# Half rounds on TensorE: the values of one group between the second and third score chunk of the next

## The chip, the cores and the metric

The kernel runs on one core of a Trainium2 chip. Its engines are TensorE (PE: matmuls into PSUM, with weight loads, PEld, beside them), VectorE (DVE), ScalarE (ACT), GpSimd (POOL) and SyncE (SP), which issues nearly all loads here. The metric is the device time of one execution in microseconds. The kernel before took 665.82 us, the median of 3 runs (665.6 to 666.0). The profiled execution took 665.59 us; its span, from the first to the last instruction, was 664.4 us.

## The reference

Two attention blocks, A and B, of the same shape, each decode one token against a cache; their outputs stand side by side in one row of 1024.

```python
B, Sq, D = 1, 1, 512
H, Sk, Dh = 32, 8192, 128
q = (x @ wq).reshape(B, Sq, H, Dh).transpose(0, 2, 1, 3)
scores = einsum("bhqd,bhkd->bhqk", q, k_cache) * (Dh ** -0.5)
p = softmax(scores)
o = einsum("bhqk,bhkd->bhqd", p, v_cache)
out = o.transpose(0, 2, 1, 3).reshape(B, Sq, H * Dh) @ wo      # for A and for B
```

All arrays are bf16. The caches are 4 x 64 MB, the weights 4 x 4 MB, and each byte of them is used once.

## The kernel before, in words

The 64 heads (32 of A, then 32 of B) are worked off in 16 groups of four heads (NM = 16). For a group, the keys of four heads fill one half of `kn` (8 MB: 32 partitions per head, 256 key rows per partition, in four chunks of 64), and the values fill `vn` (8 MB). `kn` has two halves that alternate from group to group, `vn` has one.

**Scores.** Keys lie with the key rows on partitions, so the score is not a matmul over the head's dimension. DVE multiplies a chunk of keys by the broadcast query in place (L421, four per group, count `s_mul`). PE then adds up the products by identity matmuls into one PSUM bank per chunk: 16 matmuls of 512 columns, L253 and L256, which leave 8 partial sums per key. DVE reduces those to scores (L426, count `s_sr`), takes the maximum (L437, L445: `gm`), and ACT computes the exponentials into `pt` and their sums into `rsum` (L378 to L383, count `s_p`).

**Values.** PE sums `rsum` over partitions (L295), waits for the values (`s_v`), multiplies `pt` with them in 64 matmuls (L304, `acc`), and counts `s_pv`. ACT copies `acc` to SBUF (L376), PE selects the four heads' parts (L310, `tps`, count `s_turn`), and DVE scales them into `oD` (L442). The program calls group n's score chunks and the values of the group behind, n-1, one round.

**The order on PE.** PE runs a loop of 17 rounds. Round n does the four chunks of group n, each as soon as its multiply is done, and then the values of group n-1. In round 16 there are no chunks; their place takes the projection of the first 48 heads by `wo` (L263 to L292), and then come the values of group 15. After the loop the last heads of B are projected, four matmuls per head (L229, `yrow`), as their pieces of `wo` arrive.

**The order on DVE.** Per group: four multiplies, four reduces, maximum, reciprocal (needs the values' L295 of group n-1), the scaling into `oD` (needs `s_turn` of group n-1), `gm`. After the last group it spreads the outputs for the projection (L457) and copies what PE returns.

**The order of loads on SP** is one queue: keys n+1 wait for the first multiply of group n (`s_mul`), values n wait for the end of the values n-1 (`s_pv`), in turn:

```python
for n in range(2, NM - 1):
    load_k(n + 1, (s_mul, NCH * n + 1))
    load_v(n, (s_pv, n + 1))
load_wo(0, 0, H, s_woA, (s_mul, NCH * (NM - 1) + 1))
load_wo(1, *WOB[0], s_wo[0])
```

Then come the values of group 15, as 6 MB (`s_v`) and 2 MB (`s_v1`), after `s_pv` of group 14, and the rest of B's `wo` in pieces of 1 MB down to 128 KB.

Of the kernel before, what the change touches and what calls it, by code (L numbers as in the profile page):

```python
# [6 lines left out]
ALU = mybir.AluOpType  # L7
# [7 lines left out]
def bass_concat_heads__mha_block_cached__gqa_block_cached__decode_kernel(  # L15
# [31 lines left out]
    NM = NA * QA  # L47
# [4 lines left out]
    NCH = T // CT  # L52
# [15 lines left out]
    with ExitStack() as st:  # L68
# [5 lines left out]
        def flat(ap):  # L74
            return ap.rearrange("p t d -> p (t d)")
# [134 lines left out]
        def got_wo(e, g):  # L210
            e.wait_ge(s_wo[g], 16)


        e = nc.tensor
        rq = e.alloc_register("pe_rq")
        n1, k1, rv, ko = [e.alloc_register("pe_" + x) for x in ("n1", "k1", "rv", "ko")]
        nc.br("pe_first", engines=[nc.tensor.engine])
        with nc.body("pe_main", valid_engines=[nc.tensor.engine]):
            tp = Count(t_pe)

            def relayout(psv, z, n):
                return e.matmul(psv[:, 0:n], zb[:, z, :], jsel[n][:], start=True, stop=True)

            def rows(g):
                h0, n = WOB[g]
                for j in range(h0, h0 + n):
                    for i in range(NQ):
                        m = QR - QR * (i % 2) + i % 2
                        r = e.matmul(yrow[i * QR:i * QR + m, 0:P], oz[:, j - HT, QR - m:QR],  # L229
                                     wo_sb[:, H + j, i * P:(i + 1) * P], start=False,  # L230
                                     stop=(j == H - 1), skip_group_check=True)
                return r

            e.reg_mov(n1, 1)
            e.reg_mov(k1, 1)
            e.reg_mov(ko, 0)
            e.wait_ge(s_qc, 2 * NA * QA + QC)

            def chunk(off):
                v = e.snap(ko, min_val=0, max_val=2 * T * Dh - CT * Dh)  # L240
                return flat(kn[:])[:, bass.ds(v + off, CT * Dh)].rearrange(
                    "p (t d) -> p t d", d=Dh)[:, :, 0:DW]

            with e.Fori(0, NM + 1) as n:
                nr = e.alloc_register("pe_nr")
                e.reg_sub(nr, n1, 1)
                with e.If_lt(nr, NM):
                    with e.Fori(0, NCH) as c:
                        e.wait_ge(s_mul, k1)
                        e.wait_ge(s_sr, k1)  # L250
                        e.reg_add(k1, k1, 1)
                        o = big[:, bass.ds(c, 1), :].rearrange("p o (t d) -> p (o t) d", d=DW)
                        e.matmul(o, ident[:], chunk(0), start=True, stop=False, skip_group_check=True)  # L253
                        with e.Fori(0, RL):
                            for u in range(RU):
                                i = e.matmul(o, ident[:], chunk((1 + u) * DW), start=False,  # L256
                                             stop=(u == RU - 1), skip_group_check=True)
                            i.then_inc(s_red, 1)
                            e.reg_add(ko, ko, RU * DW)
                        e.reg_add(ko, ko, CT * Dh - RU * RL * DW)  # L260
                    e.reg_alu(ko, ko, 2 * T * Dh - 1, op=ALU.bitwise_and)
                with e.Else():
                    e.wait_ge(t_dve, 1)  # L263
                    tp.of(relayout(zps, 0, 32))
                    e.wait_ge(t_dve, 2)
                    tp.of(relayout(z2, 1, 16))
                    jo = e.alloc_register("pe_jo")
                    e.reg_mov(jo, 0)
                    for a, c in ((0, s_woA), (1, s_wo[0])):
                        y = big[0:1, a, :]  # L270
                        e.wait_ge(t_dve, 3 + a)
                        e.wait_ge(c, 16)
                        e.matmul(y, zero[:], wo_sb[:, 0, :], start=True, stop=False,
                                 skip_group_check=True)
                        with e.Fori(0, 8 - 4 * a):
                            h = e.snap(jo, min_val=0, max_val=H + HT - 4)
                            for u in range(4):
                                i = e.matmul(y, o2[:, bass.ds(h + u, 1)], wo_sb[:, h + u, :], start=False,  # L278
                                             stop=False, skip_group_check=True)
                            i.then_inc(s_y, 1)  # L280
                            e.reg_add(jo, jo, 4)
                    e.wait_ge(t_act, 2)
                    for i in range(NQ):
                        m = QR - 1 if i % 2 else 0
                        r = e.matmul(yrow[i * QR:(i + 1) * QR, 0:P], hot[:, m:m + QR],
                                     part[:, i * P:(i + 1) * P], start=True, stop=False,
                                     skip_group_check=True)
                    e.wait_ge(t_dve, 5)
                    tp.of(relayout(zps, 0, 8))
                    e.wait_ge(t_dve, 6)  # L290
                    tp.of(relayout(z2, 1, 4))
                    e.wait_ge(t_dve, 8)  # L292
                with e.If_ne(nr, 0):
                    e.wait_ge(s_p, n1)
                    e.matmul(misc[:, 0:G], ones_f[:], rsum[:], start=True, stop=True).then_inc(s_sum, 1)  # L295
                    e.reg_alu(rv, nr, 4, op=ALU.logical_shift_left)
                    e.wait_ge(s_v, rv)
                    for j in range(T // NT):
                        if j * NT == VCUT:
                            with e.If_eq(nr, NM):  # L300
                                e.wait_ge(s_v1, 16)
                        q = QB * (j % NP)
                        ts = slice(j * NT, (j + 1) * NT)
                        i = e.matmul(acc[q:q + NT * G, :], pt[:, ts, :].rearrange("p t g -> p (t g)"),  # L304
                                     vn[:, ts, :].rearrange("p t d -> p (t d)"), start=(j < NP),
                                     stop=(j >= T // NT - NP), skip_group_check=True)
                    i.then_inc(s_pv, 1)
                    e.wait_ge(s_acc, n1)
                    for t in range(NT):
                        i = e.matmul(tps[:, 0:G], acc_sb[:, t * Dh:(t + 1) * Dh],  # L310
                                     tsel[:, t * G:(t + 1) * G], start=(t == 0), stop=(t == NT - 1))
                    i.then_inc(s_turn, 1)
                e.reg_add(n1, n1, 1)
            got_wo(e, 1)
            rows(1)
            got_wo(e, 2)
            rows(2)
            e.wait_ge(t_dve, 9)
            for g in range(3, len(WOB)):
                got_wo(e, g)  # L320
                i = rows(g)
            tp.of(i)
            nc.br("pe_end", engines=[nc.tensor.engine])
# [32 lines left out]
        e = nc.scalar  # L356
        rq, n1 = [e.alloc_register("act_" + x) for x in ("rq", "n1")]
# [38 lines left out]
        e = nc.vector  # L396
        n1, k5, rk, kt, ks = [e.alloc_register("dve_" + x) for x in ("n1", "k5", "rk", "kt", "ks")]
# [16 lines left out]
        with e.Fori(0, NM):  # L414
            e.wait_ge(s_k, rk)
            kv = e.snap(kt, min_val=0, max_val=T)  # L416
            n = e.snap(n1, min_val=1, max_val=NM) - 1
# [100 lines left out]
```

## Time and profile before

| | before |
|---|---|
| median of 3 runs | 665.82 us (665.6 to 666.0) |
| profiled execution | 665.59 us, span 664.4 us |
| PE matmul, DVE, ACT busy | 60%, 51%, 12% of the span |
| DMA queue q1 | 285.22 MB, 99.4% of 16 engines' span |
| mean granted PE clock | 0.805 |
| chain of waits | DMA 82%, DVE 12%, issue 3%, PE 2% |

In the views of the profile a row of the timeline has the start and the length in us, the engine, the line, the operation, output and input; in brackets stands the idle time before and what ended it. A row of a stretch has start and end, its length, the busy time of PE, PEld, DVE, ACT and POOL with the count of instructions, the mean granted clock of PE (1.00 is full), the share of the 16 DMA engines, and GB/s. DMA shares over short stretches are uneven, since one packet is up to 64 KB. A row of DMA issues gives the size of one and the median time from issue to landing. The chain of waits gives start, length and what was waited for.

### The profile page before, as it was taken

How to read it: one execution, taken by the hardware profiler on the slowest of the kernel's cores; microseconds unless marked ns; L12 is line 12 of the kernel's file. 1: busy time of each engine (PE TensorE's matmuls, PEld its weight loads, DVE VectorE, ACT ScalarE, POOL GpSimd, SP SyncE). 2: the span in 40 equal slices, each digit the busy share in tenths (PEclk: the TensorE clock that was granted, in tenths of full speed). 3: DMA queues.
4: the chain of work that ended last, by engine and by line, in shares of the span. 5: the costliest groups of instructions: out<-in, count | busy, mean ns of one | idle time of the engine just before them, and what ended most of it. 6: DMA issues, size and time to landing. Idle time of an engine off the chain costs nothing.

```text
span 664.4 us, 8052 instructions
## 1 busy us (share of the span) xinstructions
PE 396.2 (60%) x2406; PEld 164.9 (25%) x2406; DVE 335.9 (51%) x213; ACT 80.9 (12%) x182; POOL 2.4 (0%) x13
## 2 busy tenths in 40 slices
PE   0739576739194673919467391946739194673986
PEld 0213232313032231303223130322313032231332
DVE  1047939356280935628093662809266380926600
ACT  1320211100202010020201002020100202010030
POOL 1000000000000000000000000000000000000000
PEclk9968796959688695958869595886959598695997
DMA  9999999999999999999999999999999999999998
GB/s 378 444 442 442 422 399 442 442 442 442 442 430 414 418 442 442 442 442 442 422 399 442 442 442 442 442 434 406 422 442 442 442 442 442 422 399 442 440 424 335
DMA packets 6207, 285.24 MB, mean 429 GB/s; under 512 B 699, under 2 KB 1214, under 8 KB 1342
## 3 DMA queue, kind: packets, MB, share of 16 engines
q1 hardware_dynamic: 6200, 285.22, 99.4%
q8 instruction: 1, 0.02, 0.0%
q10 hardware_dynamic: 6, 0.00, 0.0%
HBM read 285.21 MB, written 0.00 MB: 429 GB/s over the span
## 4 chain that ended last, share of the span: by engine, by line
DMA 82%; DVE 12%; issue 3%; PE 2%; SPq 1%; DVEq 0%
DMA kn<-in_B_k_cache_dram 41%; DMA kn<-in_A_k_cache_dram 37%; DVE kn L421 11%; DMA kn<-in_B_wo_dram 4%; PE big L256 1%; SPq L173 1%; PE acc L304 1%; DVE s_sb L426 0%; DVEq L416 0%; DVEq L421 0%; PE big L253 0%; PE misc L295 0%; DVE out_q L481 0%; PE yrow L229 0%; DVEq L429 0%
## 5 line engine op out<-in xcount | busy, mean ns | idle before, releaser
L421 DVE TENSOR_TENSOR kn<-kn,qbc x64 | 278.9, 4421 | 158.5 <-DMA kn<-in_A_k_cache_dram 86.6
L256 PE MATMUL big<-kn,ident 128*128 x960 | 267.9, 421 | 0.0
L253 PE MATMUL big<-kn,ident 128*128 x64 | 27.5, 429 | 223.7 <-DVE kn L421 209.8
L256 PEld LDWEIGHTS big<-kn,ident 128*128 128x128 bf16 x960 | 101.1, 105 | 152.9 <-issue 104.4
L426 DVE TENSOR_REDUCE s_sb<-big 128x64 f32<-128x512 f32 x64 | 41.2, 686 | 64.0 <-PE big L256 64.0
L376 ACT COPY acc_sb<-acc 128x512 f32<-128x512 f32 x16 | 9.4, 585 | 476.8 <-PE acc L304 476.7
L253 PEld LDWEIGHTS big<-kn,ident 128*128 128x128 bf16 x64 | 6.3, 98 | 239.4 <-issue 237.4
L304 PE MATMUL acc<-vn,pt 128*16 128x512 bf16 x1024 | 60.6, 391 | 2.9 <-DMA vn<-in_B_v_cache_dram 2.9
L382 ACT ACTIVATE pt<-s_sb,negb 32x256 bf16<-32x256 f32 x64 | 54.8, 856 | 1.3
L442 DVE TENSOR_TENSOR oD<-tps,rinv 128x4 f32 x16 | 2.6, 163 | 75.7 <-PE tps L310 75.5
L304 PEld LDWEIGHTS acc<-vn,pt 128*16 128x16 bf16 x1024 | 24.5, 91 | 31.3 <-issue 3.5
L310 PE MATMUL tps<-tsel,acc_sb 128*128 128x4 f32 x128 | 16.9, 255 | 11.0 <-ACT acc_sb L376 10.3
L346 PE MATMUL big<-vn,acc_sb 128*128 x64 | 16.7, 407 | 6.6 <-ACT qbc L371 3.6
L310 PEld LDWEIGHTS tps<-tsel,acc_sb 128*128 128x128 f32 x128 | 15.5, 191 | 19.1 <-ACT acc_sb L376 17.9
L382 ACT ACTIVATION_READ_ACCUMULATOR pt<-s_sb,negb 32x1 f32 x64 | 15.9, 248 | 0.0
L278 PE MATMUL big<-kn,o 128*1 x48 | 12.0, 377 | 0.0
L371 ACT CAST qbc<-big 32x512 f32 x16 | 9.2, 576 | 14.7 <-PE big L346 14.5
L346 PEld LDWEIGHTS big<-vn,acc_sb 128*128 x64 | 6.5, 102 | 16.5 <-issue 11.8
L295 PE MATMUL misc<-rsum,ones_f 128*128 128x4 f32 x32 | 6.0, 259 | 6.7 <-issue 6.1
L378 ACT ACTIVATE negb<-gm 128x1 f32<-128x1 f32 x16 | 3.2, 203 | 53.2 <-DVE gm L445 53.2
L332 PE MATMUL misc<-ones_bf,kn 1*128 1x128 bf16 x4 | 0.6, 302 | 13.2 <-DMA kn<-in_B_x_dram 13.2
L295 PEld LDWEIGHTS misc<-rsum,ones_f 128*128 128x128 f32 x32 | 4.8, 188 | 13.4 <-issue 13.4
(46 smaller groups left out, 36.0 us busy)
## 6 DMA issues: line engine op xcount, KB each, us to landing
vn<-in_B_v_cache_dram SPq DMA_DIRECT2D x1, 6144.0 KB, 20.6
vn<-in_A_wq_dram SPq DMA_DIRECT2D x1, 4096.0 KB, 12.4
vn<-in_B_wq_dram SPq DMA_DIRECT2D x1, 4096.0 KB, 21.4
kn<-in_A_wo_dram SPq DMA_DIRECT2D x1, 4096.0 KB, 24.3
kn<-in_B_wo_dram SPq DMA_DIRECT2D x1, 2048.0 KB, 28.9
vn<-in_B_v_cache_dram SPq DMA_DIRECT2D x1, 2048.0 KB, 25.2
kn<-in_B_wo_dram SPq DMA_DIRECT2D x1, 1024.0 KB, 27.2
kn<-in_B_wo_dram SPq DMA_DIRECT2D x1, 512.0 KB, 28.0
```

The costliest lines, as they stand in the source:

```text
L253: e.matmul(o, ident[:], chunk(0), start=True, stop=False, skip_group_check=True)
L256: i = e.matmul(o, ident[:], chunk((1 + u) * DW), start=False, stop=(u == RU - 1), skip_group_check=True)
L278: i = e.matmul(y, o2[:, bass.ds(h + u, 1)], wo_sb[:, h + u, :], start=False, stop=False, skip_group_check=True)
L295: e.matmul(misc[:, 0:G], ones_f[:], rsum[:], start=True, stop=True).then_inc(s_sum, 1)
L304: i = e.matmul(acc[q:q + NT * G, :], pt[:, ts, :].rearrange("p t g -> p (t g)"), vn[:, ts, :].rearrange("p t d -> p (t d)"), start=(j < NP ...
L310: i = e.matmul(tps[:, 0:G], acc_sb[:, t * Dh:(t + 1) * Dh], tsel[:, t * G:(t + 1) * G], start=(t == 0), stop=(t == NT - 1))
L346: i = e.matmul(big[:].rearrange("p (u v) (i d) -> p u v i d", v=2, d=Dh)[:, bass.ds(u, 1), v].rearrange("p o i d -> p (o i) d"), xb[:, a, ...
L371: e.copy(qbc[q, bass.ds(j * 4, 4), :].rearrange("p i d -> p (i d)"), big[q, hh, :]).then_inc(s_qc, 2)
L376: e.copy(acc_sb[:], acc).then_inc(s_acc, 1)
L382: i = e.activation(pt[q, :, h], s_sb[q, :], AF.Exp, bias=negb[q, :], scale=scale, accum_out=rsum[q, h:h + 1])
L421: e.tensor_tensor(k, k, qbc[:, bass.ds(n, 1), :].broadcast_to([P, CT, Dh]), ALU.mult).then_inc(s_mul, 1)
L426: e.tensor_reduce(s_sb[:, c * CT:(c + 1) * CT], big[:, c, :].rearrange("p (t d) -> p t d", d=DW), AX.X, ALU.add).then_inc(s_sr, 1)
```

## The change

PE's loop has 33 half rounds instead of 17 rounds. A half round does two score chunks. After every second half round but the first two, that is behind chunks 0 and 1 of group n, the values of group n-1 follow, and then chunks 2 and 3 of group n. The last half round holds the projection and the values of group 15, as the last round did. The counters that told the round (`nr`, `n1`) are now registers that are counted up: `cb` the bank, `rv` the count for the values, `odd` whether values follow. What is computed, the buffers and the other engines' programs stay as they were.

```diff
-            e.reg_mov(n1, 1)
+            e.reg_mov(n1, 2)
             e.reg_mov(k1, 1)
+            e.reg_mov(rv, 16)
             e.reg_mov(ko, 0)
+            e.reg_mov(cb, 0)
+            e.reg_mov(odd, 2)
...
-            with e.Fori(0, NM + 1) as n:
-                nr = e.alloc_register("pe_nr")
-                e.reg_sub(nr, n1, 1)
-                with e.If_lt(nr, NM):
-                    with e.Fori(0, NCH) as c:
+            with e.Fori(0, 2 * NM + 1):
+                with e.If_lt(k1, NCH * NM):
+                    with e.Fori(0, NCH // 2):
                         e.wait_ge(s_mul, k1)
                         e.wait_ge(s_sr, k1)
                         e.reg_add(k1, k1, 1)
+                        c = e.snap(cb, min_val=0, max_val=NCH - 1)
...
+                        e.reg_add(cb, cb, 1)
+                        e.reg_alu(cb, cb, NCH - 1, op=ALU.bitwise_and)
...
-                with e.If_ne(nr, 0):
+                with e.If_eq(odd, 0):
                     e.wait_ge(s_p, n1)
                     e.matmul(misc[:, 0:G], ones_f[:], rsum[:], start=True, stop=True).then_inc(s_sum, 1)
-                    e.reg_alu(rv, nr, 4, op=ALU.logical_shift_left)
                     e.wait_ge(s_v, rv)
                     for j in range(T // NT):
                         if j * NT == VCUT:
-                            with e.If_eq(nr, NM):
+                            with e.If_eq(n1, NM + 1):
                                 e.wait_ge(s_v1, 16)
...
                     i.then_inc(s_turn, 1)
-                e.reg_add(n1, n1, 1)
+                    e.reg_add(n1, n1, 1)
+                    e.reg_add(rv, rv, 16)
+                    e.reg_mov(odd, 2)
+                e.reg_sub(odd, odd, 1)
```

The first place is the end of PE's inner loop over chunks, just ahead of the projection branch, in the instructions as built. Loops stand once, so the number of passes doesn't show. Before:

```order
L259 ISA
L254 COMPARE_AND_BRANCH
L260 ISA
L248 COMPARE_AND_BRANCH
L261 REGISTER_ALU
L247 UNCONDITIONAL_BRANCH
```

And in the changed kernel:

```order
L262 ISA
L257 COMPARE_AND_BRANCH
L263 ISA
L265 REGISTER_ALU
L250 REGISTER_ALU
L250 COMPARE_AND_BRANCH
L266 REGISTER_ALU
L249 UNCONDITIONAL_BRANCH
```

Two register instructions per chunk are new (the bank is counted by hand), and the inner loop's branch, L248 before and L250 now, lets through after two chunks instead of four.

The second place is the block of the values on PE, behind the projection branch, with what each instruction waits for. Before:

```order
L293 COMPARE_AND_BRANCH
L295 MATMUL misc<-rsum,ones_f 128x4 [waits s_p]
L296 REGISTER_ALU
L304 MATMUL acc<-vn,pt 16x512 [waits s_v]
L304 MATMUL acc<-vn,pt 16x512 x47
L300 COMPARE_AND_BRANCH
L300 UNCONDITIONAL_BRANCH [waits s_v1]
L304 MATMUL acc<-vn,pt 16x512 x16
L310 MATMUL tps<-tsel,acc_sb 128x4 [waits s_acc]
L310 MATMUL tps<-tsel,acc_sb 128x4 x3
L293 UNCONDITIONAL_BRANCH
L313 ISA
```

And in the changed kernel:

```order
L298 COMPARE_AND_BRANCH
L300 MATMUL misc<-rsum,ones_f 128x4 [waits s_p]
L308 MATMUL acc<-vn,pt 16x512 [waits s_v]
L308 MATMUL acc<-vn,pt 16x512 x47
L304 COMPARE_AND_BRANCH
L304 UNCONDITIONAL_BRANCH [waits s_v1]
L308 MATMUL acc<-vn,pt 16x512 x16
L314 MATMUL tps<-tsel,acc_sb 128x4 [waits s_acc]
L314 MATMUL tps<-tsel,acc_sb 128x4 x3
L317 ISA
L298 UNCONDITIONAL_BRANCH
L320 ISA
```

The block is the same, with the same waits; its branch (L293 before, L298 now) lets it run after every second pass of the outer loop, ahead of chunks 2 and 3 of the group in hand. The chunks that stood ahead of the wait on `s_v` are now behind it.

More of the change, by code (lines that the diff above doesn't have):

```diff
@@ L215, in bass_concat_heads__mha_block_cached__gqa_block_cached__decode_kernel @@
         rq = e.alloc_register("pe_rq")
-        n1, k1, rv, ko = [e.alloc_register("pe_" + x) for x in ("n1", "k1", "rv", "ko")]
+        n1, k1, rv, ko, cb, odd = [e.alloc_register("pe_" + x)
+                                   for x in ("n1", "k1", "rv", "ko", "cb", "odd")]
         nc.br("pe_first", engines=[nc.tensor.engine])
```

## The prediction

> **What bounds the kernel now.** I read the page's slices and its DMA part first, then the time by round, then the chain of waits.
>
> ```profile
> HBM read 285.21 MB, written 0.00 MB: 429 GB/s over the span
> 100.98:139.68 38.70, 22.81 (x138) 9.66 (x138) 20.71 (x12) 5.20 (x14) 0.00 (x0) 0.77 1.00 434
> 565.38:604.08 38.70, 22.81 (x138) 9.57 (x138) 20.71 (x12) 4.22 (x10) 0.00 (x0) 0.76 1.00 434
> ```
>
> The last two rows are the first and last of 13 stretches of 38.70 us, one per group: PE busy 22.8, DVE 20.7, and a DMA share of 1.00 at 434 GB/s in each. The load queue never runs dry and no engine needs 38.70 us, so the stream of caches sets the pace. The chain says the same, and shows where the engines come back into it:
>
> ```profile
> 569.84 33.97 DMA kn<-in_B_k_cache_dram
> 603.84 0.10 DVEq L416
> ...
> 634.90 27.48 DMA kn<-in_B_wo_dram
> 662.42 0.27 PE yrow L229 x3
> 662.72 0.29 DVE out_q L481
> ```
>
> Keys of the last group (15) land at 603.84. The end is the last piece of B's output weights at 662.4, and 2.0 us of work behind it. The profiled execution took 665.59 us, its span 664.4; the median of the runs is 665.82, 0.23 above it.
>
> **Part 1: the loads.** A key load waits for the first multiply of a group, which stays where it is (4.42 us after the keys land). A value load waits for the end of the values before it.
>
> ```profile
> 592.97 0.33 SPq L173 DMA_DIRECT2D vn<-in_B_v_cache_dram  x1
> 631.67 0.80 SPq L173 DMA_DIRECT2D vn<-in_B_v_cache_dram  x2
> vn<-in_B_v_cache_dram SPq DMA_DIRECT2D x7, 30.2
> vn<-in_B_v_cache_dram SPq DMA_DIRECT2D x1, 6144.0 KB, 20.6
> vn<-in_B_v_cache_dram SPq DMA_DIRECT2D x1, 2048.0 KB, 25.2
> ```
>
> Values 14 are issued at 592.97 and land 30.2 later, at 623.2, that is 19.4 us after keys 15. They are issued some 11 us before their turn on the full queue (at 603.8), and would now be issued 2 to 5 us earlier. An earlier place in a queue that is always full moves no byte: 0 us. Group 15's values (6 MB, then 2 MB, both issued from 631.67 on) land at 652.3 and 657.3 either way.
>
> **Part 2: a whole round.** Now PE does chunks 0 and 1 of group n, waits for values n-1, sums them, and only then does chunks 2 and 3.
>
> ```profile
> 618.37 0.38 PE L253 MATMUL big<-kn,ident 128*128 x1 [0.33 <-issue]
> 623.36 3.93 PE L256 MATMUL big<-kn,ident 128*128 x15
> 627.32 0.69 DVE L426 TENSOR_REDUCE s_sb<-big 128x64 f32<-128x512 f32 x1 [4.01 <-PE big L256]
> 628.00 3.63 PE L304 MATMUL acc<-vn,pt 128*16 128x512 bf16 x64
> 632.32 1.05 PE L310 MATMUL tps<-tsel,acc_sb 128*128 128x4 f32 x8 [0.69 <-ACT acc_sb L376]
> 633.59 0.16 DVE L442 TENSOR_TENSOR oD<-tps,rinv 128x4 f32 x1 [5.03 <-PE tps L310]
> 634.08 0.49 DVE L457 TENSOR_TENSOR zb<-oD,mask 128x128 bf16<-128x128 bf16 x2 [0.21 <-issue]
> 634.43 0.38 PE L222 MATMUL big<-jsel,zb 128*128 128x32 bf16 x2 [1.06 <-DVE zb L457]
> ```
>
> Before, chunk 1 is over at 618.04, chunks 2 and 3 run from 618.37 to 627.29, and only then come the values, although they landed at 623.2. In the new order PE would sit from 618.0 to 623.2, then do values (3.63), copy and selection (631.63 to 633.37: 1.74), and the two chunks (8.92). Queued behind the wait on PE are chunks 2 and 3; the DVE reduces of those chunks, its maximum and ACT's exponentials wait for them. Counted from the landing of the keys this is 19.4 + 3.6 + 1.7 + about 0.9 for the loop + 8.9 + 0.7 + 1.0 = 36.2, and 38.6 with the half clock of below, against 38.70: DVE is just free when the next keys land. Even if it is 2 us late, the next key load only slips from 4.4 to 6.4 us into a value transfer of 19.4 us. In rounds 1 to 14 the cost is 0; the cover is that transfer, and it would be gone only at about 15 us of lateness.
>
> The new half round costs a handful of register operations and one more trip through the outer loop. The trace bounds the trip: from the end of the selection (633.37) PE closed the loop, took the other branch and stood ready for the relayout at 634.43, so at most 1.05 us; at least 0. I take 0.9, since chunk set-up is in it. [...]
>
> **Part 3: the last round.** Here nothing follows to hide the lateness: A's and B's projections (one block of work on PE, from the first spread, L457, to the sum matmul, L295) start when group 14's output and chunk 3 of group 15 are done, and group 15's values come behind them.
>
> ```profile
> 635.12 8.06 PE L278 MATMUL big<-kn,o 128*1 x32
> 643.23 3.98 PE L278 MATMUL big<-kn,o 128*1 x16
> 649.09 0.38 PE L295 MATMUL misc<-rsum,ones_f 128*128 128x4 f32 x2 [0.66 <-DVE oz L474]
> 652.35 6.17 PE L304 MATMUL acc<-vn,pt 128*16 128x512 bf16 x64 [2.88 <-DMA vn<-in_B_v_cache_dram]
> 660.21 0.63 PE L229 MATMUL yrow<-kn,oz 128*32 128x128 bf16 x32
> 661.03 1.63 PE L229 MATMUL yrow<-kn,oz 128*32 128x128 bf16 x32 [0.20 <-DMA kn<-in_B_wo_dram]
> ```
>
> The block took 15.0 us (634.08 to 649.09), then PE idled 2.88 us for group 15's values. That 2.88 us, and the waits for pieces of B's weights after 661.03, are all the slack of the tail.
>
> With PE's clock up all the time: values 14 end at 623.3 + 3.63 = 626.9, selection 628.7, chunks 629.6 to 638.5, last reduce 639.2 (627.29 to 628.01: 0.72), start of the block 640.3 (0.55 for maximum and reciprocal, 0.49 from 633.59 to 634.08). That is 6.2 us later. The block ends at 655.3, the values of group 15 run 655.6 to 659.3 (both parts landed by 657.3), the rows start 1.69 later (658.52 to 660.21), at 661.0, and 64 row matmuls need 1.26 (32 in 0.63): 662.2. The last weights land at 662.4 anyway, so the change would cost nothing. All rests on the clock.
>
> **The clock.** The columns are PE, PEld, DVE, ACT, POOL busy, then the granted clock.
>
> ```profile
> 514.20:517.61 3.41, 2.37 (x36) 1.36 (x24) 0.13 (x2) 0.58 (x1) 0.00 (x0) 1.00 0.71 308
> 517.50:518.00 0.50, 0.00 (x0) 0.00 (x0) 0.27 (x2) 0.20 (x1) 0.00 (x0) 0.61 0.00 0
> 596.00:596.50 0.50, 0.00 (x0) 0.00 (x0) 0.00 (x0) 0.48 (x3) 0.00 (x0) 0.61 0.30 131
> 630.25:633.66 3.41, 2.43 (x36) 1.38 (x28) 0.07 (x1) 0.58 (x1) 0.00 (x0) 1.00 0.90 384
> 650.72:654.13 3.41, 1.78 (x20) 0.65 (x24) 0.00 (x0) 0.00 (x0) 0.00 (x0) 0.50 0.88 375
> 654.13:657.55 3.42, 3.42 (x40) 1.00 (x36) 0.00 (x0) 0.00 (x0) 0.00 (x0) 0.50 0.94 398
> 657.50:658.00 0.50, 0.50 (x16) 0.25 (x16) 0.00 (x0) 0.00 (x0) 0.00 (x0) 0.95 1.10 459
> ```
>
> A mean of 0.61 over a half microsecond puts the fall to 0.5 at 517.61 and 596.11, the 0.95 puts a rise at 657.55. These are 78.50 = 23 x 3.413 and 61.44 = 18 x 3.413 us apart: the clock is decided on a grid of 3.413 us. The stretch to 517.61 held 1.38 us of value matmuls and a selection (1.06) and was followed by a fall, that to 633.66 held about 1.42 and a selection and was not. So a window with under about 40% of dense matmuls drops the clock. Of the windows at half clock, 52% busy (650.72) did not lift it and a full one (654.13) did.
>
> The new wait is from 618.0 to 623.2, 5.2 us with one sum matmul in it. A 3.41 us window that is 60% or more inside it exists at every phase of the grid, so values 14 start at half clock, and stay there until a full window has passed: 3.4 to 6.8 us, 5.1 in the middle. The price of half clock is in these rows. Weight loads of the values go four by four, 0.43 us apart, so 0.107 for one matmul, against 3.63/64 = 0.057 at full clock; full-width matmuls of a score chunk go 0.43 apart each:
>
> ```profile
> 653.17 0.14 PEld L304 LDWEIGHTS acc<-vn,pt 128*16 128x16 bf16 x4 [0.28 <-issue]
> 653.60 0.14 PEld L304 LDWEIGHTS acc<-vn,pt 128*16 128x16 bf16 x4 [0.28 <-issue]
> ...
> 610.09 0.15 PEld L256 LDWEIGHTS big<-kn,ident 128*128 128x128 bf16 x1 [0.28 <-issue]
> 610.52 0.15 PEld L256 LDWEIGHTS big<-kn,ident 128*128 128x128 bf16 x1 [0.28 <-issue]
> ```
>
> In 5.1 us 48 go at half clock, 16 more take 0.9: 6.0 us, which is 2.4 more (1.6 at 3.4 us of half clock, 3.2 with all 64). The rows then end at 662.2 + 2.4 = 664.6 where they ended at 662.69: **+1.9**.
>
> A second fall is likelier than not. Between chunk 3 and the projections PE does next to nothing for about 2.8 us (0.72 + 1.04, and 634.08 to 635.12), between the projections and the values for some 2.2 (647.21 to 649.09, and 0.31). A window with 2.05 us (60%) of such a gap in it drops the clock: that holds for 2.1 of the 3.41 us of phases at the one gap (3.41 + 2.8 - 2 x 2.05) and 1.5 at the other. One window at half clock costs the projections 1.4 (8 matmuls of 0.43 where 14 of 0.247 would go, 0.247 being 635.12 to 647.21 over 49) and the values 1.6 (32 where 60 would go): **+1.5**. Sum: 665.59 + 1.9 + 1.5 = 669.0, on the median's scale 669.2.
>
> **Rivals.**
> - *One fall or none, because a fall needs a window that is idle throughout:* only the 5.2 us wait is long enough, and it holds a whole window in (5.2 - 3.41)/3.41, about half, of the phases; then +1.9, 667.7, else 665.8. For it: the gap from 631.6 to 634.9 in the run before did not drop the clock. Against: the stretch to 517.61 did, with 1.38 us of matmuls in it, and the other missed by hundredths. [...]
> - *The tail has room after all (no change):* the clock stays up, or PE's chain is 2 us shorter than my sum: 665.8 to 666.9, as worked out with the clock up. For it: every row of the chain is paid just once, and the end waits for a DMA. Against: the fall at 517.61.
> - *More falls or a full 6.8 us of half clock:* 0.8 + 1.6 more, 671.6.
> - *Faster:* the earlier value loads close gaps in the stream. 285.21 MB at 434 GB/s are 657.2 us of the 662.4 that the stream took, so 5.2 us are lost in all, at the start (before groups follow in 38.70 us) and the end; if a third of that were a gap that an earlier load fills, 664.1. Against: the share of 1.00 leaves no gap in the rounds, and no load's wait outside them moves.
> - *DVE so late that keys are issued late:* it decides from 15 us of lateness on, where the sum has 0 to 2; then each of 13 rounds would grow by what goes beyond, 1 us beyond giving 679. Under 1 in 50.
>
> **How the numbers follow.** Two falls 0.42, one 0.24 (by either reason), more 0.12 (with the late keys), no change 0.17, faster 0.05. A difference below 0.2% (1.3 us) can't be told from none here. The one-fall case lies partly below that bound (its low end is +1.1), so I move 0.03: faster 0.05, same 0.20, slower 0.75. The range starts inside no change, at 666.2, and reaches to 671.2; for the likeliest case alone it is 668.2 to 670.2.
>
> **What would show it.** Right: rounds still 38.70 us, DMA share 1.00; a wait of about 5 us of PE for the values in each round, the clock at 0.5 in the values behind it; the first spread of outputs (L457 before) near 642.6 instead of 634.1; no wait for group 15's values; the chain's end on PE (values 15, selection, rows) and not on the weights' DMA. Wrong: the last weights' DMA still in front of the last rows, a round over 38.8 us, or a granted clock of 1.0 at values 14.

## The result, and the profile after

The changed kernel took 668.41 us, the median of 10 runs (667.09 to 670.98); the kernel before, beside it, 665.81 us (10 runs, 665.54 to 666.0). The ratio is 1.0038, with a 95% interval of 1.003 to 1.0047: slower by 2.6 us. The single runs lie 3.9 us apart where they lay 0.5 apart before. The profiled execution of the changed kernel is the slowest of the ten (670.98 us, span 669.6), so what follows explains 5.2 us of span, twice the median loss.

From the page of the changed kernel, its span, its DMA total and its chain of waits by engine; then, from the stretches of 38.70 us, one of the first whole rounds and the last (columns: PE, PEld, DVE, ACT, POOL busy, clock, DMA share, GB/s):

```profile
span 669.6 us, 8230 instructions
HBM read 285.21 MB, written 0.00 MB: 426 GB/s over the span
DMA 74%; PE 22%; DVE 2%; issue 1%; ACT 0%; SPq 0%; DVEq 0%
139.68:178.38 38.70, 25.25 (x138) 9.88 (x138) 20.80 (x12) 3.13 (x7) 0.00 (x0) 0.82 1.00 434
565.38:604.08 38.70, 24.12 (x138) 9.74 (x138) 20.81 (x12) 4.76 (x13) 0.00 (x0) 0.87 1.00 434
```

A round is still 38.70 us, with a DMA share of 1.00 at 434 GB/s. The loads set its pace as before; nothing is lost or won in the rounds. PE's last stretch now stands on the chain. PE's part of the tail, the stretch of the timeline that the prediction showed, after the change:

```profile
623.64 6.38 PE L308 MATMUL acc<-vn,pt 128*16 128x512 bf16 x64 [4.32 <-DMA vn<-in_B_v_cache_dram]
630.72 1.05 PE L314 MATMUL tps<-tsel,acc_sb 128*128 128x4 f32 x8 [0.70 <-ACT acc_sb L383]
632.00 0.38 PE L256 MATMUL big<-kn,ident 128*128 x1 [0.23 <-issue]
637.38 3.65 PE L259 MATMUL big<-kn,ident 128*128 x15
641.07 0.69 DVE L433 TENSOR_REDUCE s_sb<-big 128x64 f32<-128x512 f32 x1 [3.01 <-PE big L259]
642.94 0.49 DVE L464 TENSOR_TENSOR zb<-oD,mask 128x128 bf16<-128x128 bf16 x2 [0.20 <-issue]
644.16 9.84 PE L283 MATMUL big<-kn,o 128*1 x32
654.05 3.62 PE L283 MATMUL big<-kn,o 128*1 x16
659.55 0.38 PE L300 MATMUL misc<-rsum,ones_f 128*128 128x4 f32 x2 [0.67 <-DVE oz L481]
659.86 5.32 PE L308 MATMUL acc<-vn,pt 128*16 128x512 bf16 x64
666.85 1.07 PE L230 MATMUL yrow<-kn,oz 128*32 128x128 bf16 x64
```

PE waits 4.32 us for values 14, does them in 6.38 us (3.63 before), and chunks 2 and 3 of group 15 come after that. The first spread (L464) starts at 642.94, 8.86 us later than before; the block from there to the sum matmul takes 16.61 us instead of 15.01. The wait of 2.88 us ahead of group 15's values is gone, since the values have landed by then; they take 5.32 us. The rows at the end no longer wait for weights. They end at 667.92, where they ended at 662.66 (661.03 + 1.63): 5.26 us, which is the whole difference of the spans.

The clock in five half microseconds and three stages of that tail (the same columns; the clock is the sixth number after the stretch's length):

```profile
622.00:622.50 0.50, 0.00 (x0) 0.00 (x0) 0.50 (x2) 0.00 (x0) 0.00 (x0) 0.94 0.46 197
632.50:633.00 0.50, 0.50 (x3) 0.09 (x2) 0.00 (x0) 0.00 (x0) 0.00 (x0) 0.68 0.84 360
642.50:643.00 0.50, 0.00 (x0) 0.00 (x0) 0.29 (x3) 0.20 (x1) 0.00 (x0) 0.92 3.41 1475
659.50:660.00 0.50, 0.45 (x6) 0.41 (x10) 0.04 (x1) 0.00 (x0) 0.00 (x0) 0.98 1.03 418
660.00:660.50 0.50, 0.50 (x8) 0.16 (x4) 0.14 (x1) 0.00 (x0) 0.00 (x0) 0.50 0.95 358
623.60:630.10 6.50, 6.38 (x64) 2.08 (x64) 0.00 (x0) 0.02 (x1) 0.00 (x0) 0.56 1.11 479
642.90:659.80 16.90, 15.09 (x64) 5.49 (x64) 1.50 (x8) 4.67 (x11) 0.00 (x0) 0.80 0.92 393
659.80:667.90 8.10, 7.41 (x138) 3.88 (x137) 0.36 (x2) 0.59 (x1) 0.00 (x0) 0.79 0.27 93
```

A fall here is the step of the clock from 1.00 to 0.50; a mean of 0.94 over half a microsecond means 0.44 us before the step. So the means 0.94, 0.68, 0.92 and 0.98 place falls at 622.44, 632.68, 642.92 and 659.98. The first three are 10.24 us apart each, 3 x 3.413, and the last comes 17.06 behind the third, 5 x 3.413. So four falls in the tail of this run: ahead of values 14, in the middle of chunk 2, at the spread, and at group 15's values.

### The profile page after: what moved, and what is told of

Read it like the earlier page. It is cut to its first block, busy times and chain, and to the rows that moved or that the text cites. A ratio compares the mean times of both kernels' runs of the same rounds, so it can differ in the third digit from the quotient of the medians.

```text
span 669.6 us, 8230 instructions
## 1 busy us (share of the span) xinstructions
PE 431.9 (65%) x2406; PEld 173.0 (26%) x2406; DVE 337.4 (50%) x213; ACT 81.0 (12%) x182; POOL 2.4 (0%) x13
## 4 chain that ended last, share of the span: by engine, by line
DMA 74%; PE 22%; DVE 2%; issue 1%; ACT 0%; SPq 0%; DVEq 0%
DMA vn<-in_B_v_cache_dram 34%; DMA vn<-in_A_v_cache_dram 34%; PE acc L308 14%; DMA kn<-in_A_k_cache_dram 6%; PE big L259 5%; PE big L283 2%; DVE kn L428 1%; PE big L256 0%; DVE s_sb L433 0%; PE tps L314 0%; SPq L173 0%; PE yrow L230 0%; PE big L278 0%; PE misc L300 0%; ACT acc_sb L400 0%
## 5 line engine op out<-in xcount | busy, mean ns | idle before, releaser
L433 DVE TENSOR_REDUCE s_sb<-big 128x64 f32<-128x512 f32 x64 | 42.7, 687 | 248.4 <-PE big L259 248.4
L308 PE MATMUL acc<-vn,pt 128*16 128x512 bf16 x1024 | 91.2, 534 | 60.2 <-DMA vn<-in_B_v_cache_dram 30.3
L308 PEld LDWEIGHTS acc<-vn,pt 128*16 128x16 bf16 x1024 | 31.2, 117 | 113.4 <-issue 44.7
L353 PE MATMUL big<-vn,acc_sb 128*128 x64 | 18.5, 447 | 6.0 <-ACT qbc L378 3.6
L283 PE MATMUL big<-kn,o 128*1 x48 | 13.5, 447 | 0.0
```

The source lines that it names most:

```text
L353: i = e.matmul(big[:].rearrange("p (u v) (i d) -> p u v i d", v=2, d=Dh)[:, bass.ds(u, 1), v].rearrange("p o i d -> p (o i) d"), xb[:, a, ...
L433: e.tensor_reduce(s_sb[:, c * CT:(c + 1) * CT], big[:, c, :].rearrange("p (t d) -> p t d", d=DW), AX.X, ALU.add).then_inc(s_sr, 1)
```

## The experiments

Theory: the whole loss is made in the last round. Chunks 2 and 3 of group 15 stand behind a wait for values 14, which uses up the slack of the tail (the 2.88 us and the waits for weights), and PE's clock falls in the new gaps. Rival A: the loss is made in every round (by the trips, that is the passes through PE's outer loop, or by a late DVE or late loads). Rival B: the end follows the start of the projections one for one, and the clock has little part. "Unused matmuls" below are matmuls of 512 columns of ones into a bank that is free at that time; they add work and leave none out.

**The last round in the old order, the others as changed.**

```diff
                 with e.Else():
+                    e.reg_mov(odd, 0)
                     e.wait_ge(t_dve, 1)
...
+                with e.If_eq(k1, NCH * NM - 1):
+                    e.reg_add(odd, odd, 1)
                 with e.If_eq(odd, 0):
```

> Half rounds in all groups but the last: the values of group 14 stand behind all four chunks of group 15 again. Theory (the loss is made in the last round alone): the time of before, 665.8 us, within 0.4. Rival A (the half rounds cost something in every round, or push loads): 668.4, as with the change.

Measured: 666.17 us (665.57 to 667.06, 11 runs) beside 665.89, ratio 1.0004 (0.9995 to 1.0013). Fourteen rounds in the new order show no cost that can be told from none. Rival A falls.

**The reverse: only the last round in the new order.**

```diff
-            e.reg_mov(odd, 2)
+            e.reg_mov(odd, 3)
...
+                with e.If_eq(k1, NCH * NM - 1):
+                    e.reg_mov(odd, 0)
                 with e.If_eq(odd, 0):
```

> The old order in all groups but the last; only the values of group 14 stand between chunks 1 and 2 of group 15. Theory: the whole loss of the change, 668.4 us, scattered over about 667 to 671 by the phase of the clock's grid. Rival A (cost in every round): 665.8 to 666.0.

Measured: 670.12 us (669.34 to 670.82, 5 runs), ratio 1.0062 (1.0048 to 1.0076), more than the full change. Its timeline says why the test was not clean:

```profile
59.25 0.38 PE L256 MATMUL big<-kn,ident 128*128 x1 [1.63 <-issue]
95.00:100.00 5.00, 4.14 (x68) 1.80 (x66) 1.29 (x3) 0.00 (x0) 0.00 (x0) 1.00 0.67 288
100.19 0.33 SPq L173 DMA_DIRECT2D vn<-in_A_v_cache_dram  x1
```

With values 0 in the old place, the new trips (1.63 us of idle PE at the first) stand ahead of them, values 1 were issued only at 100.19 (before: 96.02), and the load queue ran dry: a DMA share of 0.67 and 288 GB/s from 95 to 100 us. The last group's keys came about 2.1 us late (multiplies from 606.17 instead of 604.09). So the same edit was made again, with values 0 where the change puts them:

```diff
+                with e.If_eq(k1, NCH * 2 + 3):
+                    e.reg_add(odd, odd, 1)
+                with e.If_eq(k1, NCH * NM - 1):
+                    e.reg_mov(odd, 0)
                 with e.If_eq(odd, 0):
```

> The first try at the new order in the last round alone took 670.12 us, but its loads ran dry at 95 to 100 us, since the values of group 0 ended 4 us later than before. Here the values of group 0 stand where the change puts them, those of groups 1 to 13 behind all four chunks, those of group 14 between chunks 1 and 2 of group 15. Theory (the last round makes the whole loss): 668.4 us (667 to 671), no gap at 95 to 100. Rival A (cost in every round): 665.8 to 666.2.

Measured: 669.29 us (669.01 to 669.64, 5 runs) beside 665.82, ratio 1.005 (1.0037 to 1.0064). The loads ran without a gap (a DMA share of 0.97 and 419 GB/s from 95 to 100 us), and the values in the tail are as slow as with the change:

```profile
623.35 6.42 PE L312 MATMUL acc<-vn,pt 128*16 128x512 bf16 x64 [3.87 <-DMA vn<-in_B_v_cache_dram]
658.16 0.38 PE L304 MATMUL misc<-rsum,ones_f 128*128 128x4 f32 x2 [1.18 <-DVE oz L485]
658.47 5.32 PE L312 MATMUL acc<-vn,pt 128*16 128x512 bf16 x64
```

The new order in the last round makes the whole loss. The interval overlaps that of the full change. Of the 0.9 us by which the median lies above it, some 0.5 can be the test's own: PE sits idle 1.18 us ahead of the last sum matmul, where it is 0.67 with the change, and here two added conditions stand in the way. The rest, and the scatter of only 0.6, are open.

**The clock held up, first try.** Twenty unused matmuls stand in the wait of the last round; the second kernel has 3 more after the values, 10 ahead of the projections and 5 ahead of the partial row.

```diff
+            def fill(n):
+                for _ in range(n):
+                    e.matmul(yrow, ident[:], ones_bf[:].unsqueeze(1).broadcast_to([P, 4, P]),
+                             start=True, stop=True, skip_group_check=True)
...
+                    with e.If_eq(n1, NM):
+                        fill(20)
                     e.wait_ge(s_v, rv)
```

> The changed kernel with 20 matmuls of 512 columns, whose result is not used, ahead of the wait for the values of group 14 (20 x 0.216 = 4.3 us of a wait of 4.3), so that TensorE is not idle there. Theory (the half clock makes the loss): the first fall of the clock goes, 1.9 less; later falls stay for some phases: 666.5 us (665.8 to 668). Rival B (the chain of the last round is too long even at full clock): 668.4, no gain.

> As the run before, and matmuls without use also in the three shorter gaps of TensorE in the last round: 3 while ACT copies the values of group 14, 10 ahead of the projections, 5 while ACT copies the partial row. Theory: no fall of the clock at all behind chunk 1 of group 15, 665.8 to 666.4 us, and the scatter of the runs shrinks from 3.9 to about 1 us. Rival B (chain too long at full clock): 668 or more.

Measured: 666.83 us (666.53 to 667.73, 11 runs), ratio 1.0016 (1.0007 to 1.0025), with one fall (at 642.35) left between 618 and 647 us in the profiled run; and 667.22 us (666.95 to 667.56, 11 runs), ratio 1.002 (1.0011 to 1.0029), where both batches of values took 3.63 us, as at full clock. Most of the loss went with the first twenty matmuls. The second kernel missed its expectation (665.8 to 666.4), though its scatter shrank as foretold. Part of what was left came from the fillers: in the second kernel the ten matmuls held back the relayout behind the spread (L223, the first matmul of the block),

```profile
640.07 2.33 PE L237 MATMUL yrow<-ones_bf,ident 128*128 128x512 bf16 x10 [1.41 <-issue]
642.24 0.20 PE L223 MATMUL big<-jsel,zb 128*128 128x32 bf16 x2
```

for it started at 642.24, though the spread ran from 640.57. And in both, the loads ran about 1 us later from the start on (the first multiply at 44.35 and 43.94 instead of 43.09).

**The clock held up, with loops for the long row, and a control.** Here the twenty are a loop of 5 x 4, with 3 ahead of the projections and 2 ahead of the partial row. The control is the kernel before with 33 unused matmuls under a condition that is never true: it runs none of them. In the changed kernel, the row of twenty:

```diff
+                    with e.If_eq(n1, NM):
+                        with e.Fori(0, 5):
+                            fill(4)
                     e.wait_ge(s_v, rv)
```

> The changed kernel with the 20 unused matmuls ahead of the wait for the values of group 14 written as a loop of 5 x 4, so that the program stays short, and only 3 ahead of the projections and 2 ahead of the partial row, so that they delay nothing. The unrolled fillers ended at 666.83 and 667.22 us with the whole load stream 0.7 to 1.3 us late from the first keys on. Theory (the clock makes the loss, the long program made the rest): 665.8 to 666.3 us. Rival B (the chain of the last round is too long even at full clock): 667 or more.

In the kernel before, the control:

```diff
                 with e.Else():
+                    with e.If_eq(n1, NM + 5):
+                        fill(33)
                     e.wait_ge(t_dve, 1)
```

> The kernel before with 33 unused matmuls in a branch that is never taken. Theory (a longer TensorE program costs a second instruction packet and about 1 us of the load stream at the start): two packets on the instruction queue, first keys at 44.2 instead of 43.1 us, 666.8 us. Rival (the length of the program does nothing; the late stream of the delayed kernels has another cause): 665.8 us.

Measured: 666.58 us (666.31 to 666.76, 11 runs), ratio 1.001 (1.0001 to 1.0019); and the control 666.58 us too (666.36 to 667.02, 11 runs), ratio 1.0011 (1.0002 to 1.002). The filled kernel missed its expectation (665.8 to 666.3) by 0.3, the control came near its own (666.8). First the timeline and the stages of the filled kernel:

```profile
620.01 4.48 PE L237 MATMUL yrow<-ones_bf,ident 128*128 128x512 bf16 x20
624.47 3.63 PE L318 MATMUL acc<-vn,pt 128*16 128x512 bf16 x64
640.94 0.49 DVE L474 TENSOR_TENSOR zb<-oD,mask 128x128 bf16<-128x128 bf16 x2 [0.20 <-issue]
656.26 3.63 PE L318 MATMUL acc<-vn,pt 128*16 128x512 bf16 x64
661.56 2.27 PE L230 MATMUL yrow<-kn,oz 128*32 128x128 bf16 x64
618.00:623.00 5.00, 5.00 (x26) 2.36 (x25) 5.00 (x3) 0.00 (x0) 0.00 (x0) 1.00 0.76 328
640.90:656.20 15.30, 14.36 (x68) 4.78 (x66) 1.51 (x8) 4.66 (x11) 0.00 (x0) 1.00 0.93 402
656.20:663.50 7.30, 6.37 (x134) 3.52 (x133) 0.36 (x2) 0.59 (x1) 0.00 (x0) 1.00 0.74 285
```

The clock is at 1.00 throughout, both batches of values take 3.63 us, and the 64 rows take 2.27 us instead of 1.07 because they wait for weights again (the chain that ended last has 5% of the span on the loads of B's weights, 4% before, and none with the change). The order on PE is the changed one, and it costs nothing beyond the control. The control applies to it, for the loop did not make its program short enough: it too has two packets on the instruction queue, and its first multiply starts at 44.33. Then the control, and the kernel before:

```profile
q8 instruction: 2, 0.03, 0.0%
44.14 4.43 DVE L428 TENSOR_TENSOR kn<-kn,qbc  x1 [40.31 <-DMA kn<-in_A_k_cache_dram]
```

```profile
q8 instruction: 1, 0.02, 0.0%
43.09 4.42 DVE L421 TENSOR_TENSOR kn<-kn,qbc  x1 [39.27 <-DMA kn<-in_A_k_cache_dram]
```

The longer program has two packets on the instruction queue instead of one, and its first multiply starts 1.05 us later. All six kernels with two packets began it at 43.94 to 44.35, the other eight at 43.02 to 43.42. So part of every kernel with a long row of unused matmuls (0.76 us in the control) is the price of the test. This means that the first try above, less 0.76, leaves 0.2 to 0.6 us.

**The delay without the new order.** The kernel before, with unused matmuls ahead of the projections: 33 and 47 in a row, and 33 as a loop of 11 x 3 (a short program).

```diff
                 with e.Else():
+                    fill(33)
                     e.wait_ge(t_dve, 1)
```

> The kernel before with 33 matmuls without use (33 x 0.216 = 7.1 us, of which 1.0 fills a wait) ahead of the projections, so that the block of projections starts 6.1 us late with the clock up. Theory: the room in the tail at full clock is 6.2 us, so 665.8 to 666.4 us. Rival B (the room is only the 2.9 us that TensorE waits for the last values): 6.1 - 2.9 = 3.2 more, 669.0.

> As the run before with 47 matmuls: the block starts 9.1 us late. Theory: 9.1 - 6.2 = 2.9 beyond the room, 668.7 us. Rival B: 6.2 more, 672.0.

```diff
                 with e.Else():
+                    with e.Fori(0, 11):
+                        fill(3)
                     e.wait_ge(t_dve, 1)
```

> The kernel before with the 33 unused matmuls ahead of the projections as a loop of 11 x 3: the block of projections starts 6 to 7.5 us late, with a short program. Theory (room of 6.2 us at full clock, and the 1.7 us of the unrolled form came from the stream): 665.8 to 666.6 us, one fall of the clock ahead of the last values included for some phases. Rival B (room of 2.9 us): 669.0.

Measured: 667.45 us (666.65 to 667.76, 8 runs), ratio 1.0026 (1.0016 to 1.0036); 669.07 us (668.78 to 671.0, 4 runs), ratio 1.0058 (1.0043 to 1.0074); and the loop 666.2 us (665.67 to 666.75, 11 runs), ratio 1.0005 (0.9996 to 1.0014). In the loop kernel PE starts the block at 640.70, 6.3 us later than the 634.43 of before (0.35 of it because its loads ran that much later), and the time does not move beyond its interval: the tail has some 6 us of room, as the prediction's full-clock sum had it, and rival B falls. With 47 matmuls the relayout starts at 644.62, 10.2 us later, and the rows end at 665.98, 3.3 later: 6.9 of the 10.2 are swallowed. The rows of before show where this room lies: the wait of 2.88 us, the 2.54 us by which the values behind it are slower than at full clock (6.17 instead of 3.63), and 1.38 us of waiting in the last 64 row matmuls (2.45 instead of 1.07), 6.80 in all. The row of 33 missed its expectation (665.8 to 666.4): of its 1.68 us the long program accounts for 0.76, as the control prices it, and some 0.9 is open. The eleven runs of the loop kernel lie between 665.67 and 666.75, twice as far apart as those of before beside it; why is open. The profiled one (666.66) is among the later and had a fall of the clock soon after its last values began: they took 5.32 us from 655.67 on, and a mean of 0.83 puts the fall at 656.33.

```profile
655.67 5.32 PE L311 MATMUL acc<-vn,pt 128*16 128x512 bf16 x64
656.00:656.50 0.50, 0.50 (x16) 0.24 (x8) 0.00 (x0) 0.00 (x0) 0.00 (x0) 0.83 0.67 279
```

**Another place for the values: behind the third chunk, and behind the first.** Both have a loop of single chunks; they differ in the first value of `odd`, which is 6 behind the third chunk and 4 behind the first.

```diff
-            e.reg_mov(odd, 2)
+            e.reg_mov(odd, 6)
...
-            with e.Fori(0, 2 * NM + 1):
-                with e.If_lt(k1, NCH * NM):
-                    with e.Fori(0, NCH // 2):
+            with e.Fori(0, NCH * NM + 1):
+                with e.If_lt(k1, NCH * NM + 1):
+                    with e.Fori(0, 1):
...
                 with e.Else():
+                    e.reg_mov(odd, 0)
...
-                    e.reg_mov(odd, 2)
+                    e.reg_mov(odd, NCH)
```

> The values of group n-1 behind the third chunk of group n instead of the second. Chunk 2 ends about when the values land (622.5 against 623.2 in the last round), so TensorE hardly waits, and only one chunk (4.8 us with its gap) is behind the values. Theory: the block of projections starts about 1.5 us late, inside 6.2 us of room: 665.8 to 666.3 us. Rival (any interleaving costs, by the loop or by the split of the chunks): 667 or more.

> The values of group n-1 behind the first chunk of group n: the wait grows, and three chunks are behind the values. Theory: rounds stay at 38.70 us although the chain within one, 41 to 44 us from the landing of the keys, is longer than a round, since each wait for values sets it back; the last round loses one chunk more: 668.4 + 4.8 = 673.2 us (672 to 675). Rival A (lateness adds up over the rounds): 3 us or more in each of 13 rounds, over 700.

Measured: 667.04 us (666.33 to 668.16, 11 runs) beside 665.77, ratio 1.0021 (1.0012 to 1.003); and 675.32 us (674.65 to 675.57, 4 runs), ratio 1.0144 (1.0129 to 1.016). Behind the third chunk, PE did not wait for values 14, and in the tail loads are waited for again:

```profile
658.72 1.04 PE L309 MATMUL acc<-vn,pt 128*16 128x512 bf16 x16 [1.56 <-DMA vn<-in_B_v_cache_dram]
662.25 1.90 PE L230 MATMUL yrow<-kn,oz 128*32 128x128 bf16 x64
```

It was still 1.3 us slower than before, which missed the expectation (665.8 to 666.3): the last group's keys came 1.27 us later than before (the multiplies start at 605.36 instead of 604.09). The likely reason, not shown by itself, is the trip of the outer loop per chunk (1.77 us of idle PE ahead of the chunk at 622.06), which delays the first groups. Behind the first chunk the rounds stayed at 38.70 us and 434 GB/s: even a whole chunk more behind the wait slows no round. That kernel pays in the tail alone, a little more than expected (672 to 675), where a third chunk and two more trips stand behind values 14 (one trip: 1.77 us of idle PE ahead of the chunk at 643.76).

No version was faster than the kernel before. In the filled kernel with the loop the rows at the end waited for weights again, so that the loads set the end.

## Why the prediction was right, and where its terms were not

It gave 669.2 us, in a range of 666.2 to 671.2, and slower with 0.75; 668.41 was measured. Its mechanism stands: free in the rounds, and paid for in the last round by PE's clock.

**Part 1, loads earlier in a full queue: 0.** Right: the share is 1.00 in the rounds and the rate 434 GB/s. The kernel with the old last round prices parts 1 and 2 together, at 0.28 us (666.17 beside 665.89), which its interval does not tell from none.

**Part 2, the rounds: 0.** Right: the rounds stay at 38.70 us. The sum, with the half clock, left DVE 0.1 us before it would be late. The waits of DVE for B's keys, before and after (wait in all, number, longest):

```profile
DVE kn L421 <- DMA kn<-in_B_k_cache_dram: 71.4, 8, 8.9
```

```profile
DVE kn L428 <- DMA kn<-in_B_k_cache_dram: 8.9, 8, 1.6
```

DVE still waits 1.1 us in the mean, so it is about 1 us short of being late. The last group's keys come 0.43 us later than before (604.52 instead of 604.09), but 0.33 of it is there at the first multiply (43.42 instead of 43.09), within the scatter of the kernels with one packet; it is not made in the rounds.

**The trip through the loop: 0.9 taken, bounds 0 to 1.05.** Wrong in size: from the selection to chunk 2, where the sum has it, the trip is 0.23 us. And 1.05 is no bound for every trip. A larger price stands at another place, where PE goes from chunk 1 to chunk 2 past the values block that it does not enter, in the group that has none:

```profile
59.06 0.38 PE L256 MATMUL big<-kn,ident 128*128 x1 [1.72 <-issue]
63.96 0.38 PE L256 MATMUL big<-kn,ident 128*128 x1 [0.72 <-DVE s_sb L433]
```

1.72 us of idle PE there; at the next chunk, inside the inner loop, 0.72, and that ended by DVE. The row that the bound of 1.05 was taken from (the relayout in the last round) goes straight through, so it bounded the wrong jump. The change pays it visibly once, in group 0, where the values that follow still end earlier than before (values 1 are issued at 88.69 instead of 96.02); the single-chunk kernels and the one with values 0 in the old place pay it more often, and there it showed. What takes the 1.72 us, no run shows.

**Part 3 with the clock up: block of projections 6.2 us later, no cost.** Right, and shown by itself. In the filled kernel the spread comes 16.47 us after the start of values 14 (624.47 to 640.94), against 17.0 in the sum; the oversized trip makes the difference. The loop kernel delays the block by 6.3 us at no cost. But the 2.88 us and the waits for weights are not all the slack, as the prediction has it: 2.54 us of the room come from group 15's values, which no longer start at half clock, and the prediction's own sum uses them.

**One half-clock spell at values 14: 2.4.** Right in kind, and near in size: 6.38 us instead of 3.63 is 2.75. The profiled execution happened to end on the dearest of three phases, which the same wait goes through in the rounds:

```profile
507.54 6.41 PE L308 MATMUL acc<-vn,pt 128*16 128x512 bf16 x64 [4.35 <-DMA vn<-in_B_v_cache_dram]
546.24 5.84 PE L308 MATMUL acc<-vn,pt 128*16 128x512 bf16 x64 [4.36 <-DMA vn<-in_B_v_cache_dram]
584.94 5.27 PE L308 MATMUL acc<-vn,pt 128*16 128x512 bf16 x64 [4.34 <-DMA vn<-in_B_v_cache_dram]
```

A round of 38.70 us is 11.34 steps of the grid of 3.413, so the phase comes back after three rounds; the mean over the 14 rounds with a wait is 5.87 us, a price of 2.24. The trip too large by 0.7, the spell too small by 0.35 and values that land some 0.3 later than in the sum nearly cancel: that the spread, forecast for 642.6, came at 642.94 is in part luck.

**A second fall: 1.5, at the projections or at the values.** In the profiled run both happened, 1.60 in the block (16.61 instead of 15.01) and 1.69 in the last values (5.32 instead of 3.63). One more, in chunk 2, cost about 0.1 net: the two chunks took 9.03 us (632.00 to 641.03) instead of 8.92, since the wait of 0.60 us for DVE ahead of chunk 3 fell away.

The price of one window at half clock was right for the values (1.6 forecast, 1.69 measured) and too high for the projections (1.4 forecast): in the kernel with the values behind the third chunk the block took 15.35 us (638.74 to 654.09) instead of 15.01, so 0.34. That the clock was down for one window there is the author's estimate, from the first 32 matmuls of the block (8.75 us instead of 8.06); one window it was in the first kernel with twenty unused matmuls (642.35 to 645.77). In the profiled run it stayed down for two windows (642.92 to 649.75). The three spells make 2.75 + 1.60 + 1.69 = 6.04 us, where 2.4 + 1.5 = 3.9 was forecast. Without them, by this sum, the chain would have ended at 667.92 - 6.04 = 661.88, close to the 662.2 of the prediction and 0.8 ahead of the old end; that is why the span shows 5.2 and not 6. The rival "more falls", 671.6, is near what this one execution shows (670.98).

The median, 668.41, lies between the prediction's one fall (667.7) and two (669.2). Ten runs spread over 3.9 us, and those of the two kernels with the clock held up over 0.6 and 0.45, which suggests that the scatter comes with the falls; but the kernel with the new order in the last round alone has falls too, and its five runs lie within 0.6. How many falls a run of the median has is not recorded: of the runs without a trace only the mean clock is known, 0.836 to 0.844 against 0.832 in the profiled one. That 669.2 lies so near the median is therefore no proof that two falls are the usual case.

**The threshold, "under about 40% of dense matmuls".** Not sharp. The prediction misread its two rows by some hundredths: PE's 2.37 us less the selection's 1.06 leave 1.31 us of values (38%) in the window that was followed by a fall, and 2.43 less 1.05 leave 1.38 (40%) in the one that was not. In the changed kernel the window 629.28 to 632.69 held the end of the values (0.74 us), the start of chunk 2 (0.69), together 42%, and the selection, and the clock fell behind it: so the share alone does not decide. This speaks all the more against the rival that asks for an idle window.

**The signs.** All that were named came: rounds at 38.70, a wait of 3.93 to 4.37 us ahead of values 1 to 14 and the clock at 0.56 over values 14, the spread near 642.6, no wait for group 15's values, and the end on PE.

## What to carry to other kernels

Before an engine that has slack is given another order, look at the last round by itself: what hides the lateness in the rounds is not there. In a chain of matmuls that was only just covered, the idle time of the new wait counted twice here, as itself (4.32 us ahead of values 14) and as the slow clock of what followed (6.38 us instead of 3.63): the first used up the slack, and the second was what the time showed. And a test that adds instructions needs a control with the same instructions that never run (here the control alone took 0.76 us more).

## What the runs showed of the hardware that was not expected

- A longer program on PE cost time without running: 33 matmuls that are never reached gave a second packet on the instruction queue, a first multiply 1.05 us later and 0.76 us in all. That the packet and the late multiply go together is seen in six kernels; whether the one delays the other, and by what path, is open.
- A pass over the block of the values without entering it left PE idle for 1.72 us in the changed kernel, 1.77 at one place in each kernel with single chunks, and 1.63 and 1.51 in the first try at the new order in the last round alone, against 0.18 to 0.23 behind a block that was entered. At two other places it was less: 1.07 with the old last round, 0.59 at another chunk with the values behind the first.
- In the first groups the load queue had little ahead: with values 1 issued 4.2 us late (100.19 instead of 96.02) it ran dry (a DMA share of 0.67 from 95 to 100 us), and some 2.1 us stayed with the kernel to the last group (multiplies from 606.17 instead of 604.09).
- The falls of the clock lie on a grid of 3.413 us in the profile after as in that before. A window with 42% of dense matmuls was followed by a fall, and one with 40% was not.
- The phase of that grid alone made 64 value matmuls behind the same wait take 5.27, 5.84 or 6.41 us in turn, against 3.63 at full clock.
- One window at half clock cost the values 1.69 us (5.32 instead of 3.63), but the block of projections, by the estimate above, only 0.34: its first 32 matmuls took 8.75 us instead of 8.06, its next 16 then 3.62 instead of 3.98.
